# A list-ordered attention and MoE kernel: the SyncE rows of its planner get other lengths and later landings

## The chip, the cores and the metric

The kernel runs on one core of one Trainium2 chip. The time is the device time of that core in microseconds (us); less is better. Its engines are told as PE (TensorE matmul; PEld is the weight load), DVE (VectorE), ACT (ScalarE), POOL (GpSimd) and SP (SyncE, which here only issues DMAs).

## What is computed

Attention with a hash mask, then a two-layer MoE block. Cut to what matters:

```python
q_bits = (np.einsum('bhsd,dk->bhsk', q, proj) > 0)          # 6 bits per row, k likewise
mask = q_bucket[:, :, :, None] == k_bucket[:, :, None, :]
scores = np.where(mask, scale * np.matmul(q, k.transpose(0, 1, 3, 2)), -1000000000.0)
attn = softmax(scores)                                       # batch 4, 8 heads, 768 rows, 64 wide
x = np.matmul(attn, v)                                       # -> 3072 x 512
h = x @ w_in                                                 # 512 x 2048
g = np.where(h > 0.0, h, np.exp(np.minimum(h, 0.0)) - 1.0)
out = g @ w_out                                              # 2048 x 512
```

## The kernel before

**Tiling.** The 3072 rows are cut into 8 chunks of 384. A chunk has 4 head pairs, so there are 32 pairs, numbered n; each pair has 6 score tiles of 128 x 768, so there are 192 score tiles, numbered g. Values are carried as two float16 halves (hi and lo), and a product takes three matmuls.

**A pair.** K and Q are loaded (`k..load`, `q..load`), scaled and split on ACT and DVE, turned by a DMA transpose (`k..tr`, line 731, and `q..tr`, line 771) and hashed: a small matmul (`q..z`, `k..z`, line 805) makes the signs, DVE turns them into bits (`..zb`, line 826), and small DMAs copy the bits next to the turned Q or K (`q..cp`, `k..cp`, line 835). Then come the scores (`s{g}`, PE, line 946: four matmuls), the row maximum (`max{g}`, DVE, line 969), the exponential (`exp{g}`, ACT, line 997), the division with the split into two halves (`hi`, `lo`, line 363), and a DMA transpose of P (`tr{g}`, line 1053), which SP issues. When the six transposed tiles of a pair have landed, PE makes P times V (`av{n}`, 36 matmuls, line 1130). The transposed P has two tiles (ring `PT`), one for each head of a pair, so the first transposes of a pair wait for the `av` of the pair before. For the first four pairs P is turned on PE instead (`flip`, line 1013) and no DMA is in the way.

**The MoE block.** Chunk ci runs while the pairs of chunk ci+1 do: 16 steps f, each with four groups of three matmuls `F{ci}.{f}` (line 1192), the activation on ACT (lines 1216 and 1220) and DVE (1223), its split, and three groups of three matmuls `S{ci}.{f}` (line 1244).

**The weights.** 32 blocks of 512 KB are loaded in the first 100 us (`w{i}load`, line 464), decoded by ACT (`w{i}top`, line 480) and DVE (`w{i}or`, line 483) and summed on PE (`w{i}sum`, line 494). Three staging slots (ring `U`) and one more (`raw`) hold them: a load waits until the block three before it in the ring is decoded.

**What sets the order.** Nothing is reordered on the chip: each engine runs its list from front to back. The lists are made when the program is built, by `Plan.order()`. It walks through all steps with assumed lengths: at each turn it takes the step that can start first, and of several that can, the one with the least due time (`due`). A step on SP has an assumed issue time (`took`) and an assumed landing: the DMA line is taken as busy for `late`, and the landing follows 1000 ns after that, plus `slow`. What reads the data is not started before that in the plan. So `took`, `late` and `slow` of a SP step change no instruction. They change where it and all that depends on it stand in the lists.

Of the kernel before, what the change touches and what calls it, by code (L numbers as in the profile page):

```python
# [34 lines left out]
NEAR = {"P": 0.0, "V": 0.0, "A": 0.0, "S": 0.0, "G": 0.0}  # L35
BACKLOG = 4500.0
VD = -40
YIELD = (900.0, 2500.0)
FULL = 240e3
STRICT = ("v",)  # L40
# [14 lines left out]

class Op:

    __slots__ = ("engs", "eng", "run", "took", "late", "due", "deps", "after", "new", "left", "next", "start", "free", "end", "slow", "bulk", "cols", "name")

    def __init__(self, **kw):  # L60
        self.start = None
# [5 lines left out]
class Plan:  # L67
# [4 lines left out]
    def add(self, engs, run, took, due, deps=(), after=(), new=(), use=(), late=0.0, slow=0.0, bulk=False, cols=128, name=""):  # L72
        o = Op(
            engs=engs, eng=None, run=run, took=dict(zip(engs, took if type(took) is tuple else (took,))), late=late, due=due, deps=[d for d in deps if d], after=[a for a in after if a],
            new=list(new), slow=slow, bulk=bulk, cols=cols, name=name,
        )
        for b in (*new, *use):
            b.users.append(o)
        self.ops.append(o)
        return o  # L80

    def seen(self, o, e):
        return o.free if o.eng == e and e != "S" else o.end

    def ready(self, o, e):
        t = o.start[e]
# [17 lines left out]
    def order(self):  # L104
        ops = self.ops
        for o in ops:
            o.left = len(o.deps) + len(o.after)
            for d in o.deps:
                d.next.append(o)
            for a in o.after:  # L110
                a.next.append(o)
        open_ = {e: [] for e in "PVAGS"}

        def opened(o):
            o.start = {e: max([0.0] + [self.seen(d, e) for d in o.deps] + [a.start for a in o.after]) for e in o.engs}
            for e in o.engs:
                open_[e].append(o)

        free = {e: 0.0 for e in open_}
        cols = 128  # L120
        dma = 0.0
        sent = []
        for o in ops:
            if o.left == 0:
                opened(o)
        done, spun = [], []
        while len(done) < len(ops):
            best = None
            for e, waiting in open_.items():
                at, some = None, []  # L130
                for o in waiting:
                    t = self.ready(o, e)
                    if t is None:
                        continue
                    t = max(t, free[e])
                    if e == "S" and o.bulk:
                        t = max(t, dma - BACKLOG)
                    if e != o.engs[0] and free[o.engs[0]] < t + YIELD[t > FULL]:
                        continue
                    some.append((t, o.due, o, e))  # L140
                if some:
                    near = min(x[0] for x in some) + NEAR[e]
                    at = min((x for x in some if x[0] <= near), key=lambda x: x[1::-1])
                if at is not None and (best is None or at[0] < best[0]):
                    best = at
            assert best is not None, [(e, [(o.name, o.due) for o in w][:6]) for e, w in open_.items()]
            t, _, o, e = best
            o.eng = e
            for x in o.engs:
                open_[x].remove(o)  # L150
            for b in o.new:
                b.slot = len(b.ring.made) % b.ring.cap
                b.ring.made.append(b)
            took = o.took[e]
            if e == "P":
                if self.spin is not None and t < SPIN[1]:
                    gap = t - max(free[e], SPIN[0]) - SPIN[2]
                    if gap > 0.0:
                        spun.append(self.spin(max(free[e], SPIN[0]), int(gap // 214.0) + 1))
                elif t < COLD:  # L160
                    took *= 1.8
                if o.cols != cols:
                    took += SWITCH
                    cols = o.cols
            if e == "S":
                if len(sent) >= 8:
                    t = max(t, sent[-8])
                dma = max(dma, t + 950.0) + o.late
                o.end = dma + 1000.0 + o.slow
                sent.append(o.end)  # L170
            else:
                o.end = t + took + o.late + SIGNAL[e]
            o.start = t
            o.free = free[e] = t + took
            o.left = None
            done.append(o)
            for x in o.next:
                x.left -= 1
                if x.left == 0:
                    opened(x)  # L180
        return sorted(spun + done, key=lambda o: o.start)
# [18 lines left out]
def lsh_attention_moe(  # L200
# [11 lines left out]
    B, H, S, D = q.shape  # L212
# [32 lines left out]
    add = plan.add  # L245
# [197 lines left out]
    def weight_ops():  # L443
# [4 lines left out]
        def one(i):  # L448
            o = int(i >= NSI)
            place = i + 1 + o  # L450
            raw = i % 4 == 0 and (place + 1) * SL <= RAW
            t = buf("raw" if raw else "U")
            d = W[:, place, :]
            di = d.bitcast(I32)
            if o == 0:
                g, kt = i // KT, i % KT
# [3 lines left out]
            due = i - 14.0 + 0.4 * o * (i - NSI)  # L460
# [2 lines left out]
                t.t = area["raw" if raw else "U"][t.slot]  # L463
                nc.sync.dma_start(t.t["in"], src)

            l = add("S", load, 460.0, due - 6, after=([first_k["q"]] if i == 2 else []) + staged[-1:], new=[t], late=1600.0, slow=1000.0, bulk=True, name=f"w{i}load")
            staged.append(l)
            if not raw:
                in_u.append(i)
# [87 lines left out]
    first_k = {}  # L557
# [33 lines left out]
    def prep_ops(ns):  # L591
# [11 lines left out]
        for n, p in zip(ns, ps):  # L603
# [6 lines left out]
            def track(o):  # L610
                regs.append(o)
                return o
# [96 lines left out]
        for x, (n, p) in enumerate(zip(ns, ps)):  # L709
# [9 lines left out]
            if kw:  # L719
                nat, K = buf(f"natk{own}"), buf("K")  # L720
                kbuf[b, p] = K

                def k_hi(e, i=i, s=s, x=x):
                    times(s["natk"][:, :, :D], i["kf"], sc.t[:, x : x + 1], e)

                def k_lo(i=i, s=s, x=x):
                    left_over(s["natk"][:, :, D:], i["kf"], sc.t[:, x : x + 1], s["natk"][:, :, :D])

                def k_tr(K=K, s=s):
                    K.t = [okp.tile([P, 2 * NC, P], F16, tag=y, name=y, bufs=NP) for y in ("K1", "K2")]  # L730
                    nc.sync.dma_start_transpose(K.t[0], flat(s["natk"]))

                def k_dup(K=K):
                    nc.vector.tensor_copy(flat(K.t[1])[:D], flat(K.t[0])[:D])

                hi = track(add("AV", k_hi, either(2 * NC * D, pointer=True), due - 1, [chain], new=[nat], use=[sc, i["kb"]], name=f"k{n}hi"))
                lo = track(add("V", k_lo, vec(2 * NC * D, 1, True), due - 1, [hi], use=[sc, i["kb"], nat], name=f"k{n}lo"))
                if n == 0:

                    def k_new(K=K):  # L740
                        K.t = [okp.tile([P, 2 * NC, P], F16, tag=y, name=y, bufs=NP) for y in ("K1", "K2")]

                    tr = turned(s["natk"], k_new, lambda K=K: K.t[0], K, nat, [lo], due, f"k{n}tr")
                    first_k["tr"] = tr[-1]
                else:
                    tr = [track(add("S", k_tr, 1700.0, due, [lo], new=[K], use=[nat], late=2100.0, name=f"k{n}tr"))]
                dup = add("V", k_dup, vec(2 * NC * P, 4), due + 3, tr, use=[K], name=f"k{n}dup")
                cps = bits_ops(
                    f"k{n}", [(0, lambda u, K=K: flat(K.t[0])[:, u * HALF : (u + 1) * HALF]), (1, lambda u, K=K: flat(K.t[0])[:, u * HALF : (u + 1) * HALF])],
                    4, 0, lambda u, K=K: flat(K.t[1])[D : D + 2 * NB, u * HALF : (u + 1) * HALF], tr, [K], due + 3, 8, n < DIRECT,  # L750
                )
                kdone[b, p] = [*tr, dup, *cps]
# [23 lines left out]
            if n == 0:  # L776
                tr = turned(s["qq"], q_new, lambda O=O: O.both, O, nat1, [lo, dup], due + 1, f"q{n}tr", (nat2,))
            else:
                tr = [track(add("S", q_tr, 1700.0, due + 1, [lo, dup], new=[O], use=[nat1, nat2], late=2100.0, name=f"q{n}tr"))]
            i["tr"] = tr  # L780
            first_k.setdefault("q", tr[-1])
        both = [ns] if w == 2 else [[n] for n in ns]
# [14 lines left out]
    def bits_ops(name, ways, quads, which, target, deps, use, due, mms, direct):  # L797
# [34 lines left out]
        for u in range(quads):  # L832

            def copy(u=u):
                nc.sync.dma_start(target(u), zb.t[u * QD : u * QD + 2 * NB])

            cps.append(add("S", copy, 760.0, due, [s], use=[zb, *use], late=100.0, name=name + "cp"))
        return cps


# [76 lines left out]
    def pair_ops(n):  # L917
# [8 lines left out]
        for at in range(2 * HC):  # L926
# [112 lines left out]
            for y, (g, t_, PT_, pt_, _) in enumerate(duo):  # L1039
# [10 lines left out]
                def trp(t_=t_, PT_=PT_, hl=hl, make=make):  # L1050
                    if make:
# [7 lines left out]
                lows[g] = [h]  # L1059
                filled.append(  # L1060
                    add(
                        "S", trp, 1650.0, g + 2.0, [l], after=[] if make else PT_.users[:1], new=[PT_] if make else [],
                        use=[hl] + ([] if make else [PT_]), late=2100.0, name=f"tr{g}",
                    )
                )
        x16, av = buf("x16"), buf("av")
# [307 lines left out]
```

## Time and profile before

| | us |
|---|---|
| time, median of 3 runs (lowest to highest) | 857.09 (855.75 to 858.48) |
| the profiled execution: its time / its span | 857.44 / 855.7 |
| PE busy | 815.4 (95% of the span) |
| DVE busy | 678.9 (79%) |
| ACT busy | 707.0 (83%) |

The median and the profiled execution differ by 0.35 us. The span runs from the first to the last instruction; 1.7 us lie around it. PE is idle for about 40 us of the span, and the profile tells for each idle time which engine's or which DMA's signal ended it. A DMA wait shows as "<-DMA" with the tile that landed.

### The profile page before, as it was taken

How to read it: one execution, taken by the hardware profiler on the slowest of the kernel's cores; microseconds unless marked ns; L12 is line 12 of the kernel's file. 1: busy time of each engine (PE TensorE's matmuls, PEld its weight loads, DVE VectorE, ACT ScalarE, POOL GpSimd, SP SyncE). 2: the span in 40 equal slices, each digit the busy share in tenths (PEclk: the TensorE clock that was granted, in tenths of full speed). 3: DMA queues.
4: the chain of work that ended last, by engine and by line, in shares of the span. 5: the costliest groups of instructions: out<-in, count | busy, mean ns of one | idle time of the engine just before them, and what ended most of it. 6: DMA issues, size and time to landing. Idle time of an engine off the chain costs nothing. (4 is left out here: it accounts for less than half of the span.)

```text
span 855.7 us, 14941 instructions
## 1 busy us (share of the span) xinstructions
PE 815.4 (95%) x5322; PEld 439.8 (51%) x5322; DVE 678.9 (79%) x1511; ACT 707.0 (83%) x1301; POOL 4.8 (1%) x24
## 2 busy tenths in 40 slices
PE   8897888998999999999999999999999999999997
PEld 3365544554554555555555555545455555555553
DVE  5868999999997877988988788889888777773232
ACT  7789999999987889988988789888888778783543
POOL 2000000000000000000000000000000000000000
PEclk9989999999999999999999999999999999999999
DMA  9769667897889589958888888958877768552101
GB/s 298 191 204 293 200 113 130 164 217 122 169 157 178 112 185 209 201 98 154 173 150 131 144 185 191 212 105 151 154 153 141 130 106 155 99 105 38 38 1 38
DMA packets 364330, 128.21 MB, mean 150 GB/s; under 512 B 339112, under 2 KB 357216, under 8 KB 364256
## 3 DMA queue, kind: packets, MB, share of 16 engines
q1 hardware_dynamic: 363952, 127.13, 72.5%
q8 instruction: 42, 0.69, 0.3%
q14 instruction: 32, 0.26, 0.1%
q10 hardware_dynamic: 304, 0.13, 0.1%
HBM read 35.65 MB, written 6.29 MB: 49 GB/s over the span
## 5 line engine op out<-in xcount | busy, mean ns | idle before, releaser
L1192 PE MATMUL h<-X,W 128*128 128x384 f16 x1536 | 312.0, 326 | 4.1 <-ACT U L1220 4.1
L1244 PE MATMUL o<-W,U 128*128 128x512 f16 x1152 | 307.0, 379 | 0.4 <-DVE U L363 0.4
L997 ACT ACTIVATE pt<-pt,nb,sg 128x768 f32<-128x768 f32 x192 | 195.8, 1021 | 41.2 <-DVE nb L986 41.0
L1192 PEld LDWEIGHTS <-W 128*128 128x128 f16 x1536 | 148.3, 97 | 141.8 <-issue 10.3
L969 DVE TENSOR_SCALAR_CACHE_REDUCE pt<-s 128x768 f32<-128x768 f32 x180 | 171.2, 951 | 16.3 <-PE s L946 15.5
L363 DVE SCALAR_TENSOR_TENSOR hl<-pt,r,hl 128x768 f16<-128x768 f32 x168 | 165.2, 1013 | 8.4 <-ACT hl L358 8.3
L1244 PEld LDWEIGHTS <-U 128*128 128x128 f16 x1152 | 110.3, 97 | 101.8 <-issue 2.8
L946 PE MATMUL s<-K,O 128*128 128x384 f16 x720 | 147.8, 327 | 9.8 <-DVE pt L969 9.2
L358 ACT ACTIVATE hl<-pt,r 128x768 f16<-128x768 f32 x168 | 148.8, 928 | 1.0 <-ACT U L358 0.5
L1223 DVE SCALAR_TENSOR_TENSOR U<-U 128x384 f32<-128x384 f32 x128 | 70.9, 554 | 51.2 <-ACT U L1220 50.8
L946 PEld LDWEIGHTS <-O 128*128 128x128 f16 (+1 forms) x768 | 72.9, 98 | 68.5 <-issue 23.3
L1216 ACT ACTIVATE U<-h,ch 128x384 f32<-128x384 f32 x128 | 73.0, 570 | 40.5 <-PE h L1192 39.4
L358 ACT ACTIVATE U<-U,sgg 128x384 f16<-128x384 f32 x128 | 78.1, 610 | 25.6 <-DVE U L1223 25.6
L363 DVE SCALAR_TENSOR_TENSOR U<-U,sgg 128x384 f16<-128x384 f32 x128 | 78.6, 614 | 22.3 <-ACT U L358 19.9
L1130 PE MATMUL av<-PT,vhl 128*64 128x384 f16 x1008 | 90.2, 327 | 6.3 <-DMA PT<-hl 6.3
L1130 PEld LDWEIGHTS <-vhl 128*64 128x64 f16 x1008 | 57.7, 110 | 37.8 <-issue 11.4
L1220 ACT ACTIVATE U<-h,ch 128x384 f32<-128x384 f32 x128 | 72.9, 570 | 0.0
L1035 DVE TENSOR_SCALAR r<-sm 128x2 f32<-128x2 f32 x84 | 13.9, 166 | 30.5 <-ACT pt L997 30.2
L997 ACT ACTIVATION_READ_ACCUMULATOR pt<-pt,nb,sg 128x1 f32 x192 | 36.9, 192 | 0.0
L1013 PE MATMUL flip<-W,pt 128*128 128x128 f32 x144 | 23.6, 287 | 2.4 <-ACT PT L358 1.6
L358 ACT ACTIVATE X<-av 128x384 f16<-128x384 f32 x28 | 13.5, 481 | 13.6 <-PE av L1130 13.4
L363 DVE SCALAR_TENSOR_TENSOR X<-av,X 128x384 f16<-128x384 f32 x28 | 15.5, 554 | 11.3 <-ACT X L358 11.3
(134 smaller groups left out, 581.3 us busy)
## 6 DMA issues: line engine op xcount, KB each, us to landing
U<-in_moe_w_in_dram SPq DMA_DIRECT2D x12, 512.0 KB
vf<-in_v_dram SPq DMA_DIRECT2D x16, 384.0 KB
U<-in_moe_w_out_dram SPq DMA_DIRECT2D x12, 512.0 KB
qst<-in_q_dram SPq DMA_DIRECT2D x30, 192.0 KB
kst<-in_k_dram SPq DMA_DIRECT2D x14, 384.0 KB
out_dram<-W SPq DMA_DIRECT2D x16, 256.0 KB
PT<-hl SPq DMA_TRANSPOSE x168
W<-in_moe_w_in_dram SPq DMA_DIRECT2D x4, 512.0 KB
```

The lines of the kernel that those rows point to most:

```text
L358: nc.scalar.activation(o, x, AF.Copy, scale=s)
L363: nc.vector.scalar_tensor_tensor(o, x, s, hi, ALU.mult, ALU.subtract)
L946: nc.tensor.matmul(s.t[:, y, :HALF], O[x][:rows, j * HC + t, :], K[x][:rows, j * NC + y * HC : j * NC + (y + 1) * HC, :].rearrange("p a b ...
L969: nc.vector.tensor_scalar(pt.t.rearrange("p (n e) -> p n e", n=2), s.t[:, :, :HALF], CLAMP, None, ALU.max, ALU.max, accum_out=m.t[:, y : y ...
L997: nc.scalar.activation(pt_.t, pt_.t, AF.Exp, bias=nb.t[:, y : y + 1], scale=sg_of(n), accum_out=sm.t[:, z : z + 1])
L1013: nc.tensor.transpose(hb.t[:, c * P : (c + 1) * P], pt_.t[:, (y * HC + c) * P : (y * HC + c + 1) * P], eye)
L1130: nc.tensor.matmul(av.t[j * D : (j + 1) * D], vs["hl"][p].t[:, j, c, vx, :], PTs[j].t[:, :, px, c, :], start=y == 0, stop=y == 3 * NC - 1,)
L1192: nc.tensor.matmul(h.t, WH[:, g * KT + t, wx, fc * P : (fc + 1) * P], xbuf[NP * ci + t].t[:, xx, :], start=t == 0 and y == 0, stop=t == KT ...
L1216: nc.scalar.activation(e.t, h.t, AF.Exp, scale=c["ch"])
L1220: nc.scalar.activation(hp.t, h.t, AF.Relu, scale=c["ch"])
L1223: nc.vector.scalar_tensor_tensor(e.t, e.t, -1.0, hp.t, ALU.add, ALU.min)
L1244: nc.tensor.matmul(banks[t][:, :DO], g16.t[:, gx, t * P : (t + 1) * P], WH[:, NSI + 1 + f, wx, :], start=f == 0 and y == 0, stop=f == NF - ...
```

## The change

Only numbers that the planner reckons with are changed, and one detail of its bookkeeping. A constant for three kinds of landing is added, in ns: transposed P, transposed K and Q, bits.

```diff
+SLACK = (1500.0, 1000.0, 500.0)
...
-            l = add("S", load, 460.0, due - 6, ... late=1600.0, slow=1000.0, bulk=True, name=f"w{i}load")
+            l = add("S", load, 500.0, due - 6, ... late=1600.0, slow=1000.0, bulk=True, name=f"w{i}load")
...
-  add("S", k_tr, 1700.0, due, [lo], ... late=2100.0, name=f"k{n}tr")
+  add("S", k_tr, 1900.0 if early else 1800.0, due, [lo], ... late=2100.0, slow=SLACK[1], name=f"k{n}tr")
...
-  add("S", q_tr, 1700.0, due + 1, [lo, dup], ... late=2100.0, name=f"q{n}tr")
+  add("S", q_tr, 2700.0 if early else 2300.0, due + 1, [lo, dup], ... late=2100.0, slow=SLACK[1], name=f"q{n}tr")
...
-            cps.append(add("S", copy, 760.0, due, [s], use=[zb, *use], late=100.0, name=name + "cp"))
+            cps.append(add("S", copy, 820.0, due, [s], use=[zb, *use], late=100.0, slow=SLACK[2], name=name + "cp"))
...
-                        "S", trp, 1650.0, g + 2.0, [l], ... late=2100.0, name=f"tr{g}",
+                        "S", trp, 1780.0, g + 2.0, [l], ... late=2100.0, slow=SLACK[0], name=f"tr{g}",
```

The rest of the diff gives a step a mark `dma` ("S" is among its engines) in place of a test for the engine's name; as all such steps are on SP alone, it does the same as before. All engines compute what they computed; a handful of splits and evictions that may run on ACT or DVE change sides (three weight halves, one Q half and one P tile leave DVE for ACT, and one half each of a weight block, of V and of Q and one P tile leave ACT for DVE). What changes is the order of the lists, at these three places above all.

**PE, pair 9, about 257 us.** Here `s` reads K, `o` is the second MoE layer, `h` the first, `av` is P times V. Before, `av9` stands right behind `s63` and `S1.4`:

```order
L946 LDWEIGHTS O
L946 MATMUL s<-K_2639,O 128x384
L946 LDWEIGHTS O
L946 MATMUL s<-K_2639,O 128x384
L1244 LDWEIGHTS U
L1244 MATMUL o<-W,U 128x512
L1244 LDWEIGHTS U
L1244 MATMUL o<-W,U 128x512
L1244 LDWEIGHTS U
L1244 MATMUL o<-W,U 128x512
L1130 LDWEIGHTS vhl
L1130 MATMUL av<-PT,vhl 64x384
```

In the change (its line numbers are one higher) it stands behind `F1.7` and `S1.5`:

```order
L1193 LDWEIGHTS W
L1193 MATMUL h<-X,W 128x384
L1193 LDWEIGHTS W
L1193 MATMUL h<-X,W 128x384
L1245 LDWEIGHTS U
L1245 MATMUL o<-W,U 128x512
L1245 LDWEIGHTS U
L1245 MATMUL o<-W,U 128x512
L1245 LDWEIGHTS U
L1245 MATMUL o<-W,U 128x512
L1131 LDWEIGHTS vhl
L1131 MATMUL av<-PT,vhl 64x384
```

Seven groups of three matmuls that stood behind `av9` now stand ahead of it: four of `F` (`F1.6` three times, `F1.7`) and three of `S` (`S1.4` twice, `S1.5`). In the same way `av7` gets six groups ahead of it (four F, two S), `av17` and `av25` eight (three F, three S and two score tiles), and `q26z` fourteen.

**SP, pairs 22 and 24, about 547 to 576 us.** The names: `PT<-hl` is a transpose of P, `O<-natq` one of Q, `K<-natk` one of K, `O<-zb` and `K<-zb` copies of bits, the rest loads. Before:

```order
L731 DMA_TRANSPOSE K_6634<-natk 128x12x128
L620 DMA kst<-in_k_dram 128x2x384
L630 DMA qst<-in_q_dram 128x2x192
L771 DMA_TRANSPOSE O<-natq 128x12x128
L1053 DMA_TRANSPOSE PT<-hl 128x12x128 x2
L835 DMA K_6511<-zb 12x384 x4
L1053 DMA_TRANSPOSE PT<-hl 128x12x128
L835 DMA O<-zb 12x384 x4
L1053 DMA_TRANSPOSE PT<-hl 128x12x128 x5
```

Now:

```order
L732 DMA_TRANSPOSE K_6659<-natk 128x12x128
L1054 DMA_TRANSPOSE PT<-hl 128x12x128 x2
L836 DMA K_6517<-zb 12x384 x4
L1054 DMA_TRANSPOSE PT<-hl 128x12x128 x2
L772 DMA_TRANSPOSE O<-natq 128x12x128
L621 DMA kst<-in_k_dram 128x2x384
L631 DMA qst<-in_q_dram 128x2x192
L1054 DMA_TRANSPOSE PT<-hl 128x12x128 x2
L836 DMA O<-zb 12x384 x4
```

The last transpose of pair 22, `tr137`, stood alone behind the four copies `q24cp`; it now follows `tr136`, and the Q transpose with its loads and the copies have gone behind both. On PE, `q24z` has gone behind `av22`, and `av22` itself comes two groups earlier (one F, one S). Pair 14, 190 us before, is changed alike.

**ACT, the front, about 32 to 48 us.** `pt<-pt` is an exponential, `X<-U` and `X<-W` the decoding of a weight block, `PT<-flip` the eviction of a turned P tile. Before:

```order
L997 ACTIVATE pt,sw<-pt,nb,sg 128x768 x3
L358 ACTIVATE PT<-flip 128x384 x2
L997 ACTIVATE pt,sw<-pt,nb,sg 128x768
L480 ACTIVATE X<-U 128x512
L997 ACTIVATE pt,sw<-pt,nb,sg 128x768
L480 ACTIVATE X<-U 128x512
L358 ACTIVATE PT<-flip 128x384
L997 ACTIVATE pt,sw<-pt,nb,sg 128x768
L480 ACTIVATE X<-U 128x512
L358 ACTIVATE PT<-flip 128x384 x4
```

Now:

```order
L998 ACTIVATE pt,sw<-pt,nb,sg 128x768 x3
L359 ACTIVATE PT<-flip 128x384 x2
L998 ACTIVATE pt,sw<-pt,nb,sg 128x768 x3
L481 ACTIVATE X<-U 128x512 x2
L359 ACTIVATE PT<-flip 128x384 x2
L481 ACTIVATE X<-U 128x512
L359 ACTIVATE PT<-flip 128x384 x2
L998 ACTIVATE pt,sw<-pt,nb,sg 128x768
```

Two exponentials have come ahead of the first of these weight blocks. On PE, the flip of tile 3 and score tile 8 have come ahead of the sum of weight block 7, for which DVE's decoding must be done. Further on, about 74 us, SP's load of weight block 22 has gone behind the transpose `q4tr`, and DVE's decoding of block 22 behind four row maxima. Behind that, the score tiles 36 and 48 stand three F and three S groups later, and score tile 60 five F and three S groups later.

## Rows read from the trace of the kernel before

**Rows 1.** Windows by stage: length, busy PE, PEld, DVE, ACT, POOL, clock, DMA.

```profile
20.00:62.00 42.00, 36.79 (x257) 20.24 (x255) 32.55 (x83) 31.45 (x63) 0.00 (x0) 0.92 0.71 192
62.00:110.00 48.00, 40.05 (x332) 26.05 (x329) 43.12 (x109) 45.38 (x93) 0.00 (x0) 1.00 0.75 232
110.00:210.00 100.00, 89.05 (x572) 46.87 (x570) 97.70 (x214) 98.85 (x180) 0.00 (x0) 1.00 0.83 156
210.00:262.00 52.00, 49.37 (x342) 26.48 (x341) 46.76 (x102) 45.69 (x82) 0.00 (x0) 1.00 0.83 159
262.00:848.00 586.00, 580.69 (x3720) 311.89 (x3721) 446.75 (x971) 468.08 (x847) 0.00 (x0) 1.00 0.70 133
```

**Rows 2.** Waits of PE, 262 to 848 us: total us, times, longest.

```profile
PE av L1130 <- DMA PT<-hl: 3.6, 3, 1.6
PE z L805 <- DMA O<-natq: 1.0, 1, 1.0
PE s L946 <- DVE pt L969: 0.3, 1, 0.3
```

**Rows 3.** Timeline of PE at the DMA waits: start, us, instruction, [idle before, releaser].

```profile
211.30 1.00 PE L1130 MATMUL av<-PT,vhl 128*64 128x384 f16 x10 [0.75 <-DMA PT<-hl]
...
258.87 1.33 PE L1130 MATMUL av<-PT,vhl 128*64 128x384 f16 x14 [1.68 <-DMA PT<-hl]
...
378.85 1.46 PE L1130 MATMUL av<-PT,vhl 128*64 128x384 f16 x15 [1.32 <-DMA PT<-hl]
...
447.55 1.65 PE L1130 MATMUL av<-PT,vhl 128*64 128x384 f16 x18 [0.72 <-DMA PT<-hl]
...
569.35 1.82 PE L1130 MATMUL av<-PT,vhl 128*64 128x384 f16 x20 [1.61 <-DMA PT<-hl]
...
612.53 0.67 PE L805 MATMUL z<-O,pjz 128*32 128x384 f16 x10 [0.99 <-DMA O<-natq]
```

**Rows 4.** The chain that ended last, in order of time: start, us, what.

```profile
565.64 3.67 DMA PT<-hl
...
576.15 0.98 PE h L1192 x6
577.13 0.67 PE o L1244 x3
...
608.71 3.78 DMA O<-natq
```

**Rows 5.** Timeline of SP's DMA issues about pair 22.

```profile
550.89 2.35 SPq L771 DMA_TRANSPOSE O<-natq  x1
...
560.72 1.46 SPq L1053 DMA_TRANSPOSE PT<-hl  x1
562.29 3.25 SPq L835 DMA_DIRECT2D O<-zb  x4
565.64 13.68 SPq L1053 DMA_TRANSPOSE PT<-hl  x5
```

**Rows 6.** Timeline of ACT in the front, the three longest idle times.

```profile
32.46 1.03 ACT L997 ACTIVATE pt<-pt,nb,sg 128x768 f32<-128x768 f32 x1 [4.36 <-DVE nb L986]
...
39.34 0.78 ACT L480 ACTIVATE X<-U 128x512 f16<-128x512 bf16 x1 [1.47 <-DMA U<-in_moe_w_in_dram]
...
47.01 0.49 ACT L358 ACTIVATE PT<-flip 128x384 f32<-128x384 f32 x1 [2.54 <-PE flip L1013]
```

**Rows 7.** Timeline of SP's DMA issues about weight block 22.

```profile
73.23 1.06 SPq L464 DMA_DIRECT2D U<-in_moe_w_out_dram  x2
...
75.56 3.74 SPq L771 DMA_TRANSPOSE O<-natq  x1
...
80.73 7.88 SPq L464 DMA_DIRECT2D U<-in_moe_w_out_dram  x3
```

**Rows 8.** Timeline of ACT where weight block 21 is decoded.

```profile
79.20 0.77 ACT L480 ACTIVATE X<-U 128x512 f16<-128x512 bf16 x1 [1.80 <-DMA U<-in_moe_w_out_dram]
```

**Rows 9.** Waits of SP, 262 to 848 us: total us, times, longest.

```profile
SPq L1053 <- PE s L946: 59.3, 20, 5.4
```

More of the change, by code (lines that the diff above doesn't have):

```diff
@@ L56 @@
 class Op:
-    __slots__ = ("engs", "eng", "run", "took", "late", "due", "deps", "after", "new", "left", "next", "start", "free", "end", "slow", "bulk", "cols", "name")
+    __slots__ = ("engs", "eng", "run", "took", "late", "due", "deps", "after", "new", "left", "next", "start", "free", "end", "slow", "bulk", "dma", "cols", "name")
     def __init__(self, **kw):
@@ L74, in add @@
             engs=engs, eng=None, run=run, took=dict(zip(engs, took if type(took) is tuple else (took,))), late=late, due=due, deps=[d for d in deps if d], after=[a for a in after if a],
-            new=list(new), slow=slow, bulk=bulk, cols=cols, name=name,
+            new=list(new), slow=slow, bulk=bulk, dma="S" in engs, cols=cols, name=name,
         )
@@ L82, in seen @@
     def seen(self, o, e):
-        return o.free if o.eng == e and e != "S" else o.end
+        return o.free if o.eng == e and not o.dma else o.end
     def ready(self, o, e):
@@ L135, in order @@
                     t = max(t, free[e])
-                    if e == "S" and o.bulk:
+                    if o.bulk:
                         t = max(t, dma - BACKLOG)
@@ L164, in order @@
                     cols = o.cols
-            if e == "S":
+            if o.dma:
                 if len(sent) >= 8:
@@ L464, in load @@
                 nc.sync.dma_start(t.t["in"], src)
-            l = add("S", load, 460.0, due - 6, after=([first_k["q"]] if i == 2 else []) + staged[-1:], new=[t], late=1600.0, slow=1000.0, bulk=True, name=f"w{i}load")
+            l = add("S", load, 500.0, due - 6, after=([first_k["q"]] if i == 2 else []) + staged[-1:], new=[t], late=1600.0, slow=1000.0, bulk=True, name=f"w{i}load")
             staged.append(l)
@@ L745, in prep_ops @@
                 else:
-                    tr = [track(add("S", k_tr, 1700.0, due, [lo], new=[K], use=[nat], late=2100.0, name=f"k{n}tr"))]
+                    tr = [track(add("S", k_tr, 1900.0 if early else 1800.0, due, [lo], new=[K], use=[nat], late=2100.0, slow=SLACK[1], name=f"k{n}tr"))]
                 dup = add("V", k_dup, vec(2 * NC * P, 4), due + 3, tr, use=[K], name=f"k{n}dup")
@@ L778, in prep_ops @@
             else:
-                tr = [track(add("S", q_tr, 1700.0, due + 1, [lo, dup], new=[O], use=[nat1, nat2], late=2100.0, name=f"q{n}tr"))]
+                tr = [track(add("S", q_tr, 2700.0 if early else 2300.0, due + 1, [lo, dup], new=[O], use=[nat1, nat2], late=2100.0, slow=SLACK[1], name=f"q{n}tr"))]
             i["tr"] = tr
@@ L1061, in pair_ops @@
                     add(
-                        "S", trp, 1650.0, g + 2.0, [l], after=[] if make else PT_.users[:1], new=[PT_] if make else [],
-                        use=[hl] + ([] if make else [PT_]), late=2100.0, name=f"tr{g}",
+                        "S", trp, 1780.0, g + 2.0, [l], after=[] if make else PT_.users[:1], new=[PT_] if make else [],
+                        use=[hl] + ([] if make else [PT_]), late=2100.0, slow=SLACK[0], name=f"tr{g}",
                     )
```

## The prediction

> **What bounds the kernel now.** I read the windows by stage first. From 262 to 848 us PE is busy 580.69 of 586.00 us at a granted clock of 1.00, its upper level of 2.4 GHz, while DVE has 447 and ACT 468 [rows 1]: two thirds of the program end when PE has done its list, and each idle us of PE there is a us of the total. The list of waits says what that idle time is: 3.6 us in three waits of `av` for a transposed P, 1.0 us in one wait of `q26z` for a transposed Q, 0.3 us for DVE [rows 2]. That is 4.9 of the 5.3 us. From 110 to 210 us it is another machine: ACT is busy 98.85 and DVE 97.70 of 100 us, PE 89.05 [rows 1]. There PE's 11 idle us are paid by the two others, and a shorter wait of PE alone buys nothing; only a hole in ACT or DVE, here or ahead, moves the end of this stage. From 210 to 262 us the three are near each other (49.4, 46.8, 45.7 of 52) and PE's 2.6 idle us hold two waits for a transposed P, 0.75 and 1.68 us [rows 1, 3]. The front, 20 to 62 us, has holes everywhere: ACT 10.6, DVE 9.4, PE 5.2 of 42 us [rows 1].
>
> The late stage rests on PE's being truly full. The trace shows six matmuls of 384 columns in 0.98 us [rows 4], 0.163 us each, which is 384 columns at 2.4 GHz with next to nothing between. By the Trainium skill (Perfetto Trace Analysis, Identifying the Most-Contended Engine) matmul busy time is no measure here, and the share of the weight loads is to be taken: that is 312 of 586 us, 53%, which would leave PE much room and make these waits worth nothing. The rate of the matmuls speaks against it, and the measurement decides.
>
> **The waits after 262 us.** A transpose of P lands 3.67 us after its issue begins and one of Q 3.78 us [rows 4], and the `av` that waits has been listed too near to that. The change lists it later or the transpose earlier.
> - `av17` waits 0.72 us [rows 3]. Now three F, three S and two score groups stand ahead of it. Three h matmuls take half of 0.98 us, 0.49, and three o matmuls 0.67 us [rows 4]; a score group has four of the same width, 0.65. That is 1.5 + 2.0 + 1.3 = 4.8 us of ready work ahead of a wait of 0.72. The wait goes.
> - `q26z` waits 0.99 us [rows 3] and goes back by fourteen groups. The wait goes. The score tiles that need its bits stand further back in PE's list, so nobody else is kept.
> - `av14` and `av22` wait 1.32 and 1.61 us [rows 3] and come earlier, by an F, an S and a z group, 0.49 + 0.67 + 0.67 = 1.8 us. What helps them is SP: `tr137` was issued at 565.64, behind the copies that hold SP from 562.29 on, and `tr136` at 560.72 took 1.46 us [rows 5]. Directly behind `tr136` it starts at about 562.3 and lands at 562.3 + 3.67 = 566.0. The first matmul of `av22` was due at 569.35 - 1.61 = 567.7, with 1.8 us taken off 565.9. So the wait goes, or 0.1 us of it stays; that `q25tr`, 2.35 us of SP's time [rows 5], also goes behind `tr137`, gives more room. I take both waits as gone and keep 0.7 us each as an upper bound for what stays.
> - On the other side, `q16z` and `q24z` no longer stand ahead of score tiles 91 and 139, and the second waited for DVE's maximum in spite of that, for 0.3 us [rows 2]. If DVE is no earlier, these two waits grow by the z group, up to 0.7 us each: 0 to +1.5. I take 0, since the rows of DVE ahead of that maximum are reordered too.
> - A later `av` also holds its P tiles longer. The first transpose of the next pair waits for that already now, 59.3 us of SP's waits in 20 times [rows 9], and behind it on SP stand that pair's other transposes and the bits. From one `av` to the next there are 23.8 us (211.30 to 258.87 is two pairs [rows 3]). Six transposes at about 1.5 us [rows 5], a landing of 3.7 and the 3 us of the `av` need 16; 4.8 us of delay fit into the remaining 8. I cost it at nothing. If that cover were gone, each moved `av` would wait for the rest of the shift of the one before.
>
> Sum of this stage: -3.6 - 1.0 = **-4.6 us**, with ends at -4.9 and -1.7 (0.7 twice and 1.5 given back).
>
> **210 to 262 us.** `av7` gets four F and two S groups ahead of it (3.3 us against a wait of 0.75) and `av9` four F and three S (4.0 us against 1.68). Both waits go, but DVE and ACT are at 90 and 88% here [rows 1] and can set the pace in PE's place. Ends 0 and -2.4; I take half, **-1.2 us**.
>
> **The front.** ACT's longest holes are 4.36 us before the first exponential, 1.47 before a weight block that has not landed and 2.54 before the eviction of flip 3 [rows 6]. The first stays: the same DVE work stands ahead of the bias that ends it. The second is now filled by two exponentials, and the third closes because flip 3 has gone ahead of a weight sum on PE. ACT is nearly full from 62 us on (45.4 of 48, then 98.85 of 100 [rows 1]), so what it gains by 62 us would last until 210. That is up to 2.54 + 1.47 = 4.0 us. Against it stand later weight blocks, since ACT and DVE now do attention first. The load of block 22 was the second issue from 73.23 and was out by 74.29; now it goes behind `q4tr`, which holds SP until 79.30 [rows 7]: 5 us later. Its staging slot serves block 26 (in the 80.73 row), and that one's slot block 30. A load here takes 6.0 us from its issue to the decoding (73.23 to 79.20, and ACT waited 1.80 us for it [rows 7, 8]), so the delay can be handed on, and ACT would meet up to 4 us of it at the last blocks near 105 us. Ends -4.0 and +4.0. I take **-1.0 us**, nearer to the gain of flip 3 than to the loss, because the decodings are listed later as well.
>
> One rule bears on the weights. Rows show a P transpose landing after 3.7 us when nothing large is ahead of it [rows 4], and here SP's issue alone of `q4tr` takes 3.74 us among the 512 KB loads [rows 7]. By the Trainium skill (DMA: Bandwidth & Descriptors, Queues, rings and completion order) each DMA engine takes the descriptors of its ring in order, so a small transfer lands after the large ones ahead of it, and one constant per kind cannot tell its landing. By that the front's waits for DMAs would stay as they are, and this term would be 0 instead of -1.0.
>
> **The sum.** Made against the profiled execution: 857.44 - 4.6 - 1.2 - 1.0 = 850.64. The median of the runs lies 0.35 lower, so the forecast is 850.3 us. The ends of all terms together are -4.9 - 2.4 - 4.0 = -11.3 and -1.7 - 0 + 4.0 = +2.3, which is 845.8 and 859.4 at the median. The final MoE chunk, behind the last `av`, stands as before and costs nothing new.
>
> **Rivals.**
> 1. *The front closes both holes and nothing sets the pace in PE's place.* The saturated stage carries it: 857.1 - 4.6 - 2.4 - 4.0 = 846.1. For it: ACT at 98.85%. Against it: DVE is nearly as full and must gain the same.
> 2. *The weight chain eats the gain.* ACT loses 4 us near 105 us through slots 22, 26 and 30: 857.1 - 4.6 - 1.2 + 4.0 = 855.3, within what can't be told from no change. For it: the hole of 1.80 us that ACT already has for block 21 [rows 8].
> 3. *The waits only move.* The planner's clock is not the chip's; `av` moved by eight groups may meet a P tile held too long, and new waits of the same size appear: 856.5.
> 4. *Slower.* In the stage where ACT and DVE are full, score tiles 36 and 48 are moved behind three F and three S groups (3 x 0.49 + 3 x 0.67 = 3.5 us each) and tile 60 behind five F and three S (4.5 us), because bits are reckoned to land later. If DVE has nothing else to do while PE works through these, it loses up to 11.5 us at places where it has 2.3 idle us in 100 [rows 1]: 857.1 - 5.8 + 11.5 = 862.8. It decides from 8.4 us on, three quarters of the price, since 5.8 us are gained elsewhere and 2.6 must show. Against it: the list of DVE puts other splits ahead of these maxima, and the moved F groups give ACT and DVE work.
>
> **How the numbers follow.** A difference of 0.3% (2.6 us) is about what a measurement of this kernel can tell from no change. Forecast with its own range of 847 to 853.5: 0.60. Rival 1: 0.14. Rival 2: 0.10. Rival 3: 0.06. Rival 4: 0.10. Faster than 854.5 are the forecast and rival 1, 0.74; within 0.3% are rivals 2 and 3, 0.16; slower 0.10. The range for 8 in 10 takes the lower end of the sum, 845.8 rounded down, and reaches above past rivals 2 and 3, to 857.5.
>
> **What would show it.** In the profile after, the waits of PE from 262 us on should list at most 1 us for P or Q transposes, and PE's idle time in those 586 us should fall from 5.3 to about 1. `tr137` should be issued within 2 us of `tr136`, and `av22` should not wait. ACT's hole before the eviction of flip 3 should be under 0.5 us, and the window from 110 to 210 us should again show ACT and DVE at 97% and more. I am wrong if PE's waits for DVE's maximum grow by as much as the DMA waits fall, if ACT gets holes before the decoding of blocks 22, 26 or 30, or if exponentials 36, 48 and 60 wait for their bias.

## The result and the profile after

The changed kernel takes 843.56 us (median of 4 runs, 842.22 to 845.32), the kernel before beside it 856.78 us (855.75 to 858.48): a ratio of 0.9845, 95% interval 0.982 to 0.987. That is 13.2 us less. The forecast was 850.3 us, with a range down to 845.5: the direction is right, the gain is about twice what was forecast, and the time lies below the range. The profiled execution took 845.32 us, with a span of 843.6 (855.7 before).

The windows by stage, in the columns of [rows 1]; the last one ends at 836 because the program is shorter:

```profile
20.00:62.00 42.00, 38.78 (x279) 22.04 (x280) 34.20 (x89) 33.10 (x66) 0.00 (x0) 0.96 0.73 201
62.00:110.00 48.00, 39.88 (x323) 25.20 (x323) 42.95 (x108) 46.29 (x96) 0.00 (x0) 1.00 0.78 234
110.00:210.00 100.00, 90.84 (x569) 47.15 (x566) 97.81 (x211) 98.58 (x181) 0.00 (x0) 0.97 0.79 153
210.00:262.00 52.00, 52.00 (x364) 27.86 (x363) 47.73 (x106) 47.13 (x84) 0.00 (x0) 1.00 0.87 158
262.00:836.00 574.00, 573.82 (x3697) 307.77 (x3696) 445.19 (x969) 466.70 (x844) 0.00 (x0) 1.00 0.71 136
```

From 210 to 836 us PE is shown idle for 0.2 us in all. The list of PE's waits for 262 to 836 us, which held the three rows of [rows 2], is empty. From 110 to 262 us it held these three at the head before:

```profile
PE s L946 <- DVE pt L969: 6.1, 6, 1.5
PE h L1192 <- ACT U L1220: 4.1, 4, 1.2
PE av L1130 <- DMA PT<-hl: 2.6, 3, 1.7
```

The third is the waits of `av7`, `av8` and `av9`. Now no DMA is left in it:

```profile
PE s L947 <- DVE pt L970: 8.0, 5, 2.4
PE h L1193 <- ACT U L1221: 0.9, 1, 0.9
PE o L1245 <- DVE U L364: 0.2, 1, 0.2
```

Where [rows 3] showed an `av` or a `z` cut in two by a wait, the timeline of PE after has one whole group each (av9, av17, av22, q26z; start, us, instruction):

```profile
258.06 3.12 PE L1131 MATMUL av<-PT,vhl 128*64 128x384 f16 x36
...
444.34 3.12 PE L1131 MATMUL av<-PT,vhl 128*64 128x384 f16 x36
...
556.91 3.12 PE L1131 MATMUL av<-PT,vhl 128*64 128x384 f16 x36
...
611.32 0.67 PE L806 MATMUL z<-O,pjz 128*32 128x384 f16 x12
```

On SP, where [rows 5] had the copies and 2.35 us of `q25tr` ahead of the last transposes of pair 22, two P transposes now go out in one row, with `q25tr` behind them:

```profile
549.10 4.25 SPq L1054 DMA_TRANSPOSE PT<-hl  x2
553.45 1.46 SPq L772 DMA_TRANSPOSE O<-natq  x1
```

ACT's longest holes in the front are now these; of the three in [rows 6] the first is as it was, the second has shrunk and the one before the eviction of flip 3 is gone, with a new one ahead of an exponential:

```profile
33.28 1.03 ACT L998 ACTIVATE pt<-pt,nb,sg 128x768 f32<-128x768 f32 x1 [4.35 <-DVE nb L987]
43.18 0.79 ACT L481 ACTIVATE X<-U 128x512 f16<-128x512 bf16 x1 [0.61 <-DMA U<-in_moe_w_in_dram]
46.66 1.03 ACT L998 ACTIVATE pt<-pt,nb,sg 128x768 f32<-128x768 f32 x1 [1.61 <-DVE nb L987]
```

Weight block 22 goes out 4 us later than in [rows 7], behind `q4tr`, and ACT waits 0.84 us for it:

```profile
74.01 4.06 SPq L772 DMA_TRANSPOSE O<-natq  x1
78.17 0.99 SPq L465 DMA_DIRECT2D U<-in_moe_w_out_dram  x2
```

```profile
84.63 0.78 ACT L481 ACTIVATE X<-U 128x512 f16<-128x512 bf16 x1 [0.84 <-DMA U<-in_moe_w_out_dram]
```

**Where the 13 us are.** The stage borders fall on different work in the two lists. Three marks on PE have exactly the same groups ahead of them in both: the first group of F0.10 (177.07 us before, 177.76 after), of F2.0 (315.88, 311.46) and of F7.0 (784.60, 772.19). Between the last two the kernels run the same 3036 matmuls. Windows of the kernel before between the marks, and of the kernel after:

```profile
0.00:177.07 177.07, 151.41 (x1053) 84.76 (x1054) 152.71 (x366) 158.73 (x308) 4.76 (x24) 0.98 0.79 201
177.07:315.88 138.81, 134.10 (x883) 71.36 (x881) 121.05 (x269) 122.13 (x224) 0.00 (x0) 1.00 0.82 157
315.88:784.60 468.72, 463.41 (x3036) 249.30 (x3035) 384.65 (x845) 394.82 (x715) 0.00 (x0) 1.00 0.78 148
```

```profile
0.00:177.76 177.76, 154.67 (x1054) 85.45 (x1058) 153.11 (x365) 160.46 (x312) 4.76 (x24) 0.97 0.79 204
177.76:311.46 133.70, 132.49 (x883) 70.48 (x881) 121.58 (x270) 121.41 (x222) 0.00 (x0) 1.00 0.83 157
311.46:772.19 460.73, 460.66 (x3036) 247.54 (x3034) 383.68 (x841) 395.16 (x714) 0.00 (x0) 1.00 0.79 151
```

The first stretch is 0.7 us longer, which is less than two executions of one list differ by there (177.76 us here, 175.21 in another execution of the changed kernel); the second is 5.1 shorter, the third 8.0. In the third, PE's idle time falls from 5.31 to 0.07 us, which is 5.2. The other 2.75 us are busy time: the same matmuls at the same clock are shown 2.75 us shorter. The reason stands in rows of the kernel before that the prediction does not read. Here is av14, whose wait is in [rows 3], with the matmul ahead of the wait, and two groups, av26 and q24z, that no list names as waiting:

```profile
377.18 0.35 PE L1130 MATMUL av<-PT,vhl 128*64 128x384 f16 x1
378.85 3.08 PE L1130 MATMUL av<-PT,vhl 128*64 128x384 f16 x35 [1.32 <-DMA PT<-hl]
...
555.41 0.83 PE L805 MATMUL z<-O,pjz 128*32 128x384 f16 x12
...
663.32 3.50 PE L1130 MATMUL av<-PT,vhl 128*64 128x384 f16 x36
```

The 35 matmuls behind the wait take 3.08 / 35 = 0.09 us each in the mean, from the start of one to that of the next. One by itself is shown longer, 327 ns in the mean of all 1008 (the row of the page of before: count, busy us in all, mean ns of one, idle us before them):

```profile
L1130 PE MATMUL av<-PT,vhl 128*64 128x384 f16 x1008 | 90.2, 327 | 6.3 <-DMA PT<-hl 6.3
```

So they overlap as they are shown. The one ahead of a wait has nothing that overlaps with it: its whole 0.35 us count as busy, and only what goes beyond that is listed as idle. av26 takes 3.50 us for what the row after shows in 3.12, with no idle time listed; q24z takes 0.83 for 0.67. From the start of a group to the start of what follows, less the idle time, nine groups between the marks are too long by 0.23 to 0.35 us in this way (av12, av14, av17, av22, av26, q16z, q18z, q24z, q26z): 2.8 us.

### The profile page after: what moved, and what is told of

It reads as the page before. It is cut to its first block, busy times and chain, and to the rows that moved or that the text cites. A ratio compares the mean times of both kernels' runs of the same rounds, so it can differ in the third digit from the quotient of the medians.

```text
span 843.6 us, 14947 instructions
## 1 busy us (share of the span) xinstructions
PE 814.4 (97%) x5322; PEld 437.9 (52%) x5325; DVE 678.9 (80%) x1510; ACT 708.3 (84%) x1302; POOL 4.8 (1%) x24
## 4 chain that ended last, share of the span: by engine, by line
PE 77%; DVE 13%; ACT 5%; issue 2%; DMA 1%; SPq 1%; POOL 0%; DVEq 0%; ACTq 0%; POOLq 0%
PE o L1245 27%; PE h L1193 26%; PE s L947 12%; PE av L1131 9%; DVE pt L970 3%; DVE hl L364 2%; DVE W L364 2%; ACT pt L998 1%; PE z L806 1%; PE av L1101 1%; ACT X L481 1%; DMA U<-in_moe_w_out_dram 1%; PE spin L1338 1%; DVE U L1224 1%; DMA K<-zb 1%
## 5 line engine op out<-in xcount | busy, mean ns | idle before, releaser
L1131 PE MATMUL av<-PT,vhl 128*64 128x384 f16 x1008 | 87.4, 327 | 0.0
L1131 PEld LDWEIGHTS <-vhl 128*64 128x64 f16 x1008 | 55.3, 110 | 32.2 <-issue 9.3
L1338 PE MATMUL spin<-ones 128*128 128x512 bf16 x81 | 23.0, 417 | 2.6 <-POOL ones L370 2.4
L987 DVE TENSOR_SCALAR nb<-m,sg 128x2 f32<-128x2 f32 x96 | 21.9, 228 | 3.1
```

The lines of the kernel that those rows point to most:

```text
L1131: nc.tensor.matmul(av.t[j * D : (j + 1) * D], vs["hl"][p].t[:, j, c, vx, :], PTs[j].t[:, :, px, c, :], start=y == 0, stop=y == 3 * NC - 1,)
L1338: nc.tensor.matmul(x, ones, ones[:, :1].to_broadcast([P, 512]), start=True, stop=True)
```

## The experiments

Theory A: each wait of PE for a transposed tile costs its listed idle time and some 0.3 us more, shorter waits are not listed at all, and from 177 us on these waits are worth their whole length. Theory B: the waits are worth what the list says, and the rest of the gain comes from the front and from the stage in which ACT and DVE are full.

**Parts of the change.** Each is the kernel before with one part of the new numbers.

```
- "S", trp, 1650.0 ... late=2100.0, name=f"tr{g}"
+ "S", trp, 1780.0 ... late=2100.0, slow=1500.0, name=f"tr{g}"
```

> Only the transposes of P are reckoned at 1780 ns and landing 1500 ns later; K, Q, bits and weight loads as before. Theory A (each wait of PE for a transposed tile costs its listed idle time and some 0.3 us more that the trace shows as a long first matmul; the P transposes carry most of the gain): the waits of av7, av9, av14, av17 and av22, 6.1 us listed, and the hidden third of a microsecond of these and of av12 and av26 go, the four waits for a transposed Q stay: about 849.5 us, 7 below the kernel before. Theory B (the waits are worth only what the list says, and the rest of the gain comes from the stage in which ScalarE and VectorE are full, through bits and issue lengths): 852 to 854.

Measured: 848.11 us, ratio 0.9882 (0.9864 to 0.9901), 9.4 us below the kernel before. From F2.0 to F7.0 it takes 461.55 us, 7.2 less, and the only waits listed there are two for DVE, 0.3 us together. The time is nearer to theory A's; that the Q waits have gone too, with no Q number changed, it did not foresee.

```
- k_tr, 1700.0 ... late=2100.0     - q_tr, 1700.0 ... late=2100.0
+ k_tr, 1900.0 if early else 1800.0 ... slow=1000.0
+ q_tr, 2700.0 if early else 2300.0 ... slow=1000.0
```

> Only the transposes of K and Q are reckoned longer and landing 1000 ns later. Theory A: the waits of q16z and q24z go with their hidden part, the P waits stay or grow, since av14 and av22 come 1.3 us earlier in TensorE's list: 855 to 858, no difference that can be told. Theory B: the same waits go, and with them half of what the full stage gains: 852 to 854.

Measured: 852.68 us, ratio 0.9943 (0.9924 to 0.9962). The time is theory B's, the late stage is A's: 466.62 us from F2.0 to F7.0, 2.1 less, because the P waits there remain, as the waits of PE from 311 to 780 us show:

```profile
PE av L1131 <- DMA PT<-hl: 4.2, 5, 1.6
```

The other gain lies ahead of F2.0, where the re-ordering had taken away av9's wait with no change of a P number.

```
- tr 1650.0, k_tr 1700.0, q_tr 1700.0, copy 760.0, load 460.0
+ tr 1780.0, k_tr 1900.0 if early else 1800.0, q_tr 2700.0 if early else 2300.0, copy 820.0, load 500.0
```

> Only the lengths of SyncE's issues are changed (P 1780, K 1800 or 1900, Q 2300 or 2700, bits 820, weights 500), no landing. Theory A: av9 and av17 move back by 1.2 and 0.7 us, the others stay or come earlier, so most waits remain: about 854. Theory B: the front and the full stage are re-ordered by the issue lengths, 850 or less.

Measured: 853.34 us, ratio 0.9945 (0.9927 to 0.9963), near theory A's number, though not by its way: from F2.0 to F7.0 it takes 464.13 us, 4.6 less, and of 4.6 us of listed waits for DMAs 2.0 are left.

```
+ tr: slow=1500.0; k_tr, q_tr: slow=1000.0; copy: slow=500.0
```

> Only the landings are later (1500, 1000, 500 ns), the lengths of issues as before. Theory A: nearly all av move back by 0.5 to 5 us, so most of the 12 to 13 us come from here: 847 or less. Theory B: only the listed waits of av and q26z go, about 851.

Measured: 850.07 us, ratio 0.9908 (0.9883 to 0.9934), which is neither. No DMA is left in PE's waits behind 311 us, but up to F2.0 the profiled execution has gained nothing: it is there at 316.15 us (with one score group fewer ahead of the mark), the kernel before at 315.88 and the changed kernel at 311.46. Which step costs it that is open; ACT is busy 41.04 of the 52 us from 210 on, against 47.13 in the changed kernel, and the granted clock is 0.88 from 20 to 62 us, against 0.96. Neither the issue lengths nor the landings alone give what both together do.

**Stages.** Behind a change in one stage the planner's list soon comes back to the order it had, so the new numbers can be switched on for a part of the program.

```
+ "S", trp, 1780.0 if g >= 60 else 1650.0, ... slow=SLACK[0] if g >= 60 else 0.0
+ K, Q and bits likewise if n >= 12; weight loads 460.0
```

> The changed numbers hold only for the P transposes from score group 60 on and for K, Q and bits from tile 12 on; everything ahead is the kernel before, everything from q12z on is listed as in the changed kernel. Theory A (a wait of TensorE costs some 0.3 us more than its listed idle time, and shorter waits are not listed at all): the part behind 320 us gains 8.0 us, as in the changed kernel: about 849. Theory B (the waits are worth their listed 4.6 us): about 852.5.

Measured: 849.83 us, ratio 0.9896 (0.9859 to 0.9933), 8.5 us below the kernel before. Windows from F0.10 to F2.0 and from there to F7.0:

```profile
175.24:314.26 139.02, 134.07 (x882) 71.34 (x881) 121.93 (x271) 122.96 (x225) 0.00 (x0) 1.00 0.83 159
314.26:774.98 460.72, 460.65 (x3036) 247.53 (x3035) 383.54 (x841) 395.03 (x714) 0.00 (x0) 1.00 0.79 150
```

The late stretch is 460.72 us with the front of before, 460.73 in the changed kernel: 8.0 us come from the late order alone, as theory A says, and the stretch ahead of it has not moved (139.02, 138.81 before).

```
+ "S", trp, 1780.0 if g >= 36 else 1650.0, ... slow=SLACK[0] if g >= 36 else 0.0
+ K, Q and bits likewise if n >= 8; weight loads 460.0
```

> The changed numbers hold from score group 36 and from tile 8 on; up to 170 us it is the kernel before. Theory A (from 177 us on TensorE's waits are worth their whole length, with the hidden part, and the front gives nothing): 857.5 - 8.0 - 5.0 = 844.5, the changed kernel's time or 0.7 us below it. Theory B (the gain of the stage in which ScalarE and VectorE are full comes from the front): 848 to 850.

Measured: 846.27 us, ratio 0.9846 (0.981 to 0.9882), 3.6 us below the run before it. The windows between the same marks:

```profile
174.14:309.38 135.24, 133.32 (x882) 70.42 (x881) 122.58 (x273) 121.48 (x223) 0.00 (x0) 1.00 0.84 160
309.38:770.05 460.67, 460.61 (x3035) 247.50 (x3034) 383.50 (x841) 394.84 (x714) 0.00 (x0) 1.00 0.79 151
```

From F0.10 to F2.0 it is 3.8 us shorter than with the late numbers alone: 3.0 of idle time and 0.75 of busy time, the waits of av7, av8 and av9 with their hidden part.

```
+ "S", trp, 1780.0 if g < 36 else 1650.0, ... slow=SLACK[0] if g < 36 else 0.0
+ K, Q and bits likewise if n < 8; weight loads 500.0
```

> The changed numbers hold only up to score group 36 and tile 8, and for the weight loads; from 320 us on it is the order of the kernel before, with its waits. Theory A: the shorter holes of ScalarE in the front do not reach the end, 0 to +1 us: 857 to 858.5. Theory B: 2 to 4 us less, 853.5 to 855.5.

Measured: 854.67 us, ratio 0.9961 (0.9943 to 0.9978), 3.7 us less, which is theory B's number. The windows put most of it behind the front:

```profile
175.74:311.54 135.80, 133.21 (x883) 71.28 (x881) 121.30 (x269) 121.28 (x220) 0.00 (x0) 1.00 0.81 155
311.54:780.62 469.08, 463.67 (x3036) 249.91 (x3035) 384.71 (x844) 395.32 (x716) 0.00 (x0) 1.00 0.77 148
```

3.0 us lie between F0.10 and F2.0. The list returns to that of before only at av12, and on the way av9 has lost its wait; av7 still waits 0.6 us. So theory A was wrong that front numbers do nothing, and B is not shown by it either: the gain is again that of a wait.

**The front by itself.** The changed kernel and the one of the run with `g >= 36` and `n >= 8`, both unedited, side by side; their lists differ only ahead of about 320 us.

> The changed kernel once more, for a comparison with the next one on the same chip: 843 to 845, some 13 us below the kernel before.

> The kernel that lists up to 170 us as before and behind it as changed, once more, beside the changed kernel. If the new order of the front (20 to 170 us) gives or takes nothing, the two agree within 2 us. If it gives what it gave alone (3.7 us below the kernel before), this one is 2 to 4 us above the changed kernel; if the trace is right by which the changed front is later at 178 us, it is 1 to 3 us below it.

Measured: 844.47 us (ratio 0.9835, 0.9808 to 0.9862) for the changed kernel, 846.93 us (0.9855, 0.9827 to 0.9883) for the one with the old front. That is 2.5 us, the same way as in the runs before (843.56 and 846.27), but the two intervals overlap: by the medians the new front gives somewhere between nothing and 2.5 us. The traces of these two runs say where it lies, from F0.10 to F2.0 (changed kernel first):

```profile
175.21:309.11 133.90, 132.69 (x884) 70.31 (x882) 121.55 (x270) 121.50 (x222) 0.00 (x0) 1.00 0.83 156
175.82:311.06 135.24, 133.33 (x882) 70.40 (x881) 122.58 (x273) 121.51 (x223) 0.00 (x0) 1.00 0.84 160
```

That is 1.3 us, and 1.5 between the first runs of the two (133.70 and 135.24). Up to F0.10 no gain can be told: 175.21 and 177.76 us with the new front, 175.82 and 174.14 with the old one.

**Putting waits back.** The changed kernel, with some `av` moved up in PE's list so that they must wait again; nothing else is touched.

```
+ for i in range(12, 28): move av{i} up past six groups of F, S or s
```

> The changed kernel with av12 to av27 each moved up in TensorE's list by six groups of F, S or s (3.44 to 3.64 us), nothing else. In the changed kernel the last transposed P of these landed 1.32 to 3.63 us ahead of its av, so 15 of the 16 must now wait, 20.8 us in all: 864.3 by both theories. They differ in what the trace lists: by theory A some 0.3 us of each wait stand in a first matmul that is shown too long, and the listed idle time is 16 to 16.5 us; by theory B it is the whole 20.8 us.

Measured: 909.83 us, ratio 1.0599 (1.0564 to 1.0634): 66 us slower, not 21. Both theories missed; DVE now waits 70.6 us for score tiles from 320 to 760 us, where the changed kernel had 6.6 from 311 to 772. Fewer `av` and a smaller move:

```
+ for i in (14, 18, 22, 25): move av{i} up past four groups of F, S or s
```

> The changed kernel with only av14, av18, av22 and av25 moved up, by four groups of F, S or s each (2.30, 2.30, 2.30 and 2.48 us); their last P had landed 1.32, 1.62, 1.51 and 1.41 us ahead of them, so they must wait 0.98, 0.68, 0.79 and 1.07 us, 3.5 us in all, and the time between the marks F2.0 and F6.0 grows by that. Theory A (some 0.3 us of a wait stand in a first matmul that is shown too long): the trace lists 2.1 to 2.4 us of idle time for the four, and the four av are shown 0.35 us longer each. Theory B (a wait costs what is listed): 3.5 us listed. If other engines are thrown off as by the six groups of the run before, the time grows by far more.

Measured: 858.37 us in one run. From F2.0 to F7.0 it takes 475.77 us, 15.0 more than the changed kernel, though only two of the four waited: 1.2 us of idle time are listed at `av`, 9.2 in four waits for DVE, and PE is busy 4.5 us longer. PE at av14 and behind it, and DVE in the same place:

```profile
366.05 0.35 PE L1131 MATMUL av<-PT,vhl 128*64 128x384 f16 x1
367.20 3.11 PE L1131 MATMUL av<-PT,vhl 128*64 128x384 f16 x35 [0.80 <-DMA PT<-hl]
...
377.02 0.86 PE L806 MATMUL z<-O,pjz 128*32 128x384 f16 x12 [2.45 <-DVE X L364]
```

```profile
371.60 0.96 DVE L970 TENSOR_SCALAR_CACHE_REDUCE pt<-s 128x768 f32<-128x768 f32 x1 [3.97 <-PE s L947]
```

The `av` stands ahead of score group s93 now. DVE has the maximum of s93 next in its list and stops for 3.97 us, and some 8 us after its first wait PE pays a second time, 2.45 us, for what DVE has not done. The last run moves av14 and av22 as far, but keeps the score group ahead of them (PE's list at av14; av22 likewise):

```
- S2.7 F2.9 S2.7 F2.10 s93 S2.8 F2.10 av14
+ S2.7 F2.9 s93 av14 S2.7 F2.10 S2.8 F2.10
```

> The changed kernel with av14 and av22 moved up past two F and two S groups (2.3 us) as in the run before, but with the score group that stood between (s93, s141) kept ahead of the av. In the run before the av stood ahead of that score group, waited 1.1 and 0.7 us, VectorE waited up to 4.0 us for the score tile, and the stretch from F2.0 to F7.0 grew by 15.0 us. Theory C (a wait of TensorE is dear when a score group that VectorE needs next stands behind it; without that it costs its own length): the two av wait about 1.0 and 0.8 us and the stretch grows by 2 to 3 us, to 463 or 464. Theory D (any wait of that length throws the lists of the engines out of step): 8 us or more, 469 and above.

Measured: 847.06 us in one run. The waits of PE and the window from F2.0 to F7.0:

```profile
PE av L1131 <- DMA PT<-hl: 1.6, 2, 0.9
```

```profile
311.06:773.95 462.89, 461.20 (x3036) 247.78 (x3035) 384.28 (x841) 395.61 (x714) 0.00 (x0) 1.00 0.79 150
```

The stretch grows by 2.16 us for two waits: 1.6 listed, and 461.20 - 460.66 = 0.54 us of busy time, 0.27 each. It is one execution, but the five profiled executions with the late order of the changed kernel lie between 460.67 and 460.74 us here. That is theory C, and the hidden part of theory A measured with little else changed (s93 and s141 stand two groups earlier). In the group of av14 itself the hidden part is 0.35 us: the second matmul starts 1.27 us after the first, and 0.92 are listed:

```profile
367.65 0.35 PE L1131 MATMUL av<-PT,vhl 128*64 128x384 f16 x1
368.92 3.11 PE L1131 MATMUL av<-PT,vhl 128*64 128x384 f16 x35 [0.92 <-DMA PT<-hl]
```

## Why the prediction was wrong in size

- **The waits after 262 us: right mechanism, term mis-sized.** All four listed waits went, for the reasons given (ready work ahead of av17 and q26z, `tr137` directly behind `tr136` for av22), none came back through DVE at tiles 91 and 139, and later `av` cost SP nothing that PE met, although SP's own waits for PE's scores rose from the 59.3 us of [rows 9] to 69.5. The step that failed is the price: a wait was costed at its listed idle time, -4.6 us. It is 8.0: 5.2 of idle time and 2.8 that the trace books as busy PE, five of the nine waits entirely or nearly so. The sentence that PE is "truly full" when busy 580.69 of 586 us took those 2.8 us for work.
- **210 to 262 us: the half was wrong.** I took -1.2 of 2.4 us, because DVE and ACT, at 90 and 88%, could set the pace. The measured worth of the numbers for this stage is 3.6 us by the medians and 3.8 by the marks: the whole of the listed waits of av7, av8 and av9 and the hidden part. DVE and ACT were not near their limit there, they were waiting with PE: from 210 to 220 us, where av7 waited, DVE and ACT were busy 8.96 and 8.99 of 10 us before, and after it is 9.89 and 9.84. Before, ACT stood idle there until `av7` was done, and DVE until ACT was:

```profile
214.45 0.49 ACT L358 ACTIVATE X<-av 128x384 f16<-128x384 f32 x1 [1.01 <-PE av L1130]
214.97 0.56 DVE L363 SCALAR_TENSOR_TENSOR X<-av,X 128x384 f16<-128x384 f32 x1 [0.97 <-ACT X L358]
```

- **The front: not refuted.** -1.0 us was forecast, 0 to -2.5 measured by the medians and -1.3 to -1.5 by the marks, behind F0.10. Flip 3's hole closed as forecast, and block 22 came 4 us late (5 were forecast); a new hole of 1.61 us and ACT's 0.84 us for block 22, one of the signs of being wrong that the prediction names, took part of it back.
- **The sum.** 8.0 late, 3.6 in the middle and 0 to 2.5 in front are 11.6 to 14.1 us, against 13.2 measured.
- **The range** ended at 845.5 because the ends of two terms were the listed idle times. A bound from rows would have had to include the matmuls of 0.35 us ahead of each wait.
- **The rivals.** Nearest was the first (846.1), whose 4.0 us in the front are not what was found. The fourth did not come true at tiles 36, 48 and 60, with ACT and DVE as full as before from 110 to 210 us (exponentials 36 and 48, counted in ACT's list, wait under 0.1 us for their bias, exponential 60 0.81 against 0.53 before). PE's waits for DVE's maximum from 110 to 262 us did grow, from 6.1 to 8.0 us, while its waits for ACT and DMAs there fell from 6.7 to 0.9. The rival's mechanism is real, as av14 moved ahead of s93 shows: it needs a score group that DVE wants next to stand behind a PE that waits, not behind ready F and S groups.
- **The rules of the Trainium skill.** By the Trainium skill's "Perfetto Trace Analysis", Identifying the Most-Contended Engine, matmul busy time is not a good measure of how close a kernel is to its limit; the section names MFU (the work done as a share of the peak rate) beside the share of the weight loads, and the prediction took the second alone. The rival read from it, that the waits are worth nothing, is refuted by the run with `g >= 60` (8.0 us). The warning itself holds in a smaller way: 2.75 of 463.41 busy us were waiting. By the Trainium skill's "DMA: Bandwidth & Descriptors", Queues, rings and completion order, the front's term would be 0 instead of -1.0; these runs do not tell the two apart. The section says it of each DMA engine by itself; that a small transfer lands behind the whole of a large one is the prediction's own step from there.

## What to carry to other kernels

Where one engine bounds a long stage, compare the length of every group of a kind with the commonest length of that kind before adding up its waits: a group that was 0.2 to 0.4 us too long here had waited, whether a list said so or not. In a hand-ordered list the price of a wait depends on what stands behind it: with ready work of its own engine only, it cost its length here; ahead of a tile that the next engine wants, several times that. When a planner's constants are changed, switching them on for one stage at a time separates the terms better than changing one constant at a time, since each constant re-orders the whole list.

## What was not expected of the hardware

- A matmul of an `av` is shown 0.33 us long though the next one starts 0.09 us later. The one ahead of a wait counts as busy for its whole 0.35 us, so about 0.3 us of each wait of PE for a DMA is not in the list of waits (0.27 us of busy time for each of the two in the last run).
- PE's granted clock fell for some us after stretches in which it waited for other engines, in the late stage too. From 130 to 140 us, behind a wait of 2.4 us for DVE, the changed kernel shows a mean of 0.66. With av14 moved up, the four us in which PE's wait of 2.45 us for DVE ended show a mean of 0.67, between the two levels of 1.2 and 2.4 GHz:

```profile
376.00:380.00 4.00, 2.98 (x18) 1.12 (x18) 3.74 (x7) 4.00 (x10) 0.00 (x0) 0.67 0.26 49
```

In the same stretch from F2.0 to F7.0 that run has 4.5 us more of busy PE (465.19 us) than the changed kernel for the same 3036 matmuls. From 62 us on the waits of the profiled execution of before, the longest 1.68 us, left the clock at 1.00 [rows 1].
- The runs with the old front scatter by 855 to 863 us for the kernel before and 843 to 848 for the second run with `g >= 36`, the changed kernel by 842 to 845. The scatter goes with the granted clock: the kernel before took 855.93 us at a mean of 0.998 and 863.05 at 0.987, the run with `g >= 36` 843.31 at 0.999 and 848.24 at 0.993. The traces of its two runs, with one and the same list, show it in the stretch up to F0.10:

```profile
0.00:174.14 174.14, 148.74 (x1050) 82.53 (x1054) 152.73 (x366) 158.41 (x308) 4.76 (x24) 1.00 0.80 204
0.00:175.82 175.82, 152.54 (x1050) 84.41 (x1054) 152.80 (x366) 158.52 (x308) 4.78 (x24) 0.98 0.79 202
```

What makes the clock fall in one execution of a list and not in the next is not shown.
